# Last tile, one transpose and one load reordered in a fused attention and gated-MLP kernel

## Chip, cores and metric

One core of one Trainium2 chip runs the kernel. The metric is the device time of one execution in microseconds (us), lower is better. Before the change: 230.65 us, median of 3 (230.29 to 230.92). The span in a profile runs from the first to the last instruction, about 1.7 us less than the time. A program on one core has no second die to compare with, so a run of several is called slow only when it is over 1.5% above the fastest of its kernel.

## The reference

```python
x = A_x                                  # 2048 x 512, bf16
xn = layernorm(x)
# attention: 32 heads of 16, each position looks at 8 positions, 2 apart, backwards
q, k, v = split(xn @ A_wqkv)             # 512 x 1536
s = window_attention(q, k, v) @ A_wo     # 512 x 512
g = silu((gelu(xn @ B_w_gate) * (xn @ B_w_up)) @ B_w_down)   # 512 -> 1792 -> 512
return x + s * g
```

(Shortened: the mask of the first positions, the reshapes and the scale are left out.)

## The kernel before

The kernel works on four blocks of 512 rows (j = 0 to 3), each of four tiles of 128 rows. A block is normalized and transposed, projected to q, k and v, goes through attention on VectorE and the gate, up and down products on TensorE. Everything is issued by hand in an order that keeps TensorE busy. All DMAs are issued by one engine, SyncE, from one queue.

The loads at the start, and the late weights.

```python
for t in range(TPQ):                       # TPQ = 4
    load_x(t)
for i in range(3):
    load_w(wqkv_sb, A_wqkv, i * D, (i + 1) * D)      # q, k, v weights
load_x(TPQ, TPQ)
# ... gate and up weights, the other x tiles ...

def load_late_weights():
    nc.sync.dma_start(out=wd_sb[:], in_=B_w_down.rearrange("(k p) n -> p k n", p=P))
    for g in range(NC):
        nc.sync.dma_start(
            out=wo_sb[:, g, :],
            in_=bass.AP(
                tensor=A_wo.tensor, offset=g * 4 * D, ap=[[D, 4], [DH * D, H], [1, D]]
            ),
        )
```

Tiles 4 to 6 are transposed by TensorE during the first gate-and-up products, tile 7 by DMA. Then the queue loads v and the late weights:

```python
for i in range(TPQ):
    # ...
    if i < TPQ - 1:
        at(("glu", 0, i), transpose, TPQ + i)
# ...
at(("glu", 0, 0), transpose_by_dma, 2 * TPQ - 1)
at(("glu", 0, 0), load_v, 0)
at(("glu", 0, 0), load_late_weights)
```

The softmax reciprocals of blocks 0 to 2 go through DRAM, to be spread over the partitions, and are waited for by the division:

```python
def spread_by_dma(j):
    nc.sync.dma_start(out=rs_d[j][:, :], in_=st[j]["rs"][:])      # store
    rb = op.tile([P, TQ], BF16, name="rbd")
    for i in range(WL):                                           # four loads
        nc.sync.dma_start(
            out=rb[H * i : H * (i + 1), :].rearrange("h (q i) -> h q i", q=4),
            in_=rs_d[j].rearrange("(q h) i -> h q i", h=H),
        )
    st[j]["rb"] = rb
# divide(j): oT = o * rb on VectorE; down(j, tt): y = h @ wd, then s = oT @ wo
```

The last tile works by halves of the columns: y, Silu, s, multiply, add, store, twice. (Tiles named `_ps` lie in PSUM, the memory into which TensorE sums.)

The softmax here doesn't subtract the row's maximum and nothing guards it: scores larger than these inputs give would overflow.

## Time and profile before

| What | Before | How to read it |
|---|---|---|
| span | 228.8 us | first to last instruction |
| TensorE busy | 97% | the bound; VectorE 65%, ScalarE 57% |
| first q projection | 7.15 us | end of the head |
| first y and second y product of block 0 | 57.67, 61.55 us | between them is the first s product, which needs the division |
| last matmul starts | 225.24 us | end of TensorE's work |
| last store issued, landed | 226.40, 227.93 us | the tail |

The prediction shows the lines of these views: the page's busy shares and the chain that ended last, TensorE's waits, and the timelines of the head, of the queue and of the tail. The chain is followed back from the last instruction, at each step to what released it. An increment is a step of the semaphore by which a DMA says that a share of it has landed.

### The profile page before, as it was taken

The page shows a single profiled execution, that of the slowest core. Times are in us where ns is not written, and L with a number is a line of the kernel's source. Part 1 is how long each engine was busy: PE and PEld are TensorE (multiplying, and loading weights), DVE is VectorE, ACT ScalarE, POOL GpSimd, SP SyncE. Part 2 cuts the span into 40 slices and gives each one's busy share as a digit, 9 for nine tenths or more (in the row PEclk, how much of TensorE's full clock was granted, in tenths as well). Part 3 has the DMA queues.
Part 4 walks back from the last instruction along what each step waited for, and adds up shares of the span by engine and source line. Part 5 has one row for each costly group of instructions (what it writes and reads, how often), then busy time and mean ns, then how long its engine had stood idle before and what let it go on. Part 6 is the DMA issues. An engine that isn't in the chain of part 4 may idle for free.

```text
span 228.8 us, 3516 instructions
## 1 busy us (share of the span) xinstructions
PE 222.7 (97%) x1303; PEld 106.8 (47%) x1323; DVE 147.6 (65%) x234; ACT 130.6 (57%) x215; POOL 21.7 (10%) x61
## 2 busy tenths in 40 slices
PE   7999999999999999999999999999999999999994
PEld 5865444444444444444444444444444444444453
DVE  4593996894898198865678169735449429845232
ACT  3679779764514867476721687646741387647211
POOL 1048944100000000110000000000000000000000
PEclk9999999999999999999999999999999999999999
DMA  6999599922366611110266711110038910000001
GB/s 157 357 375 376 140 175 199 315 98 80 91 153 152 135 23 29 27 29 0 92 162 152 162 29 23 26 34 6 30 104 193 202 30 3 0 0 4 23 23 46
DMA packets 29857, 24.33 MB, mean 106 GB/s; under 512 B 9488, under 2 KB 29840, under 8 KB 29840
## 3 DMA queue, kind: packets, MB, share of 16 engines
q1 hardware_dynamic: 29840, 24.11, 41.0%
q8 instruction: 10, 0.16, 0.3%
q14 instruction: 7, 0.06, 0.1%
HBM read 18.61 MB, written 4.31 MB: 100 GB/s over the span
## 4 chain that ended last, share of the span: by engine, by line
PE 94%; ACT 2%; DVE 1%; DMA 1%; issue 1%; ACTq 0%; DVEq 0%
PE y_ps L411 21%; PE u_ps L242 21%; PE g_ps L242 20%; PE qkv_ps L242 17%; PE s_ps L421 6%; PE L_ps L299 3%; PE o_ps L370 3%; DMA x_sb<-in_A_x_dram 1%; PE q_ps L242 1%; PE tr L208 1%; DVE stats L177 1%; ACT L395 1%; ACT u L397 1%; PE den_ps L319 0%; ACT xnT L217 0%
## 5 line engine op out<-in xcount | busy, mean ns | idle before, releaser
L242 PE MATMUL u_ps<-xnT,wu_sb 128*128 128x512 bf16 x223 | 57.3, 379 | 0.2
L242 PE MATMUL g_ps<-xnT,wg_sb 128*128 128x512 bf16 x214 | 56.5, 379 | 0.6 <-issue 0.2
L411 PE MATMUL y_ps<-wd_sb,h 128*128 128x512 bf16 (+1 forms) x234 | 50.9, 366 | 0.2
L399 DVE TENSOR_TENSOR h<-ge,u 128x512 bf16<-128x512 bf16 x56 | 23.8, 424 | 37.5 <-ACT u L397 36.8
L288 DVE TENSOR_TENSOR pk<-q_sb,k_sb 128x2048 bf16<-128x2048 bf16 x32 | 37.8, 1221 | 7.0 <-ACT k_sb L263 7.0
L395 ACT ACTIVATE ge<-g_ps 128x512 bf16<-128x512 f32 x56 | 33.6, 600 | 14.7 <-PE g_ps L242 14.0
L397 ACT ACTIVATE u<-u_ps 128x512 bf16<-128x512 f32 x56 | 33.6, 599 | 14.6 <-PE u_ps L242 14.4
L242 PE MATMUL qkv_ps<-xnT,wqkv_sb 128*128 128x512 bf16 (+1 forms) x203 | 40.5, 354 | 0.2
L356 DVE TENSOR_TENSOR pv<-E,v_arr 128x2048 bf16<-128x2048 bf16 x32 | 38.6, 1217 | 0.0
L411 PEld LDWEIGHTS <-h 128*128 128x128 bf16 x238 | 23.3, 98 | 25.3
L418 ACT ACTIVATE sl<-y_ps 128x512 bf16<-128x512 f32 (+1 forms) x17 | 9.7, 573 | 44.0 <-PE y_ps L411 44.0
L242 PEld LDWEIGHTS <-wu_sb 128*128 128x128 bf16 x224 | 21.9, 98 | 26.6 <-issue 0.3
L242 PEld LDWEIGHTS <-wg_sb 128*128 128x128 bf16 x224 | 21.2, 98 | 26.8 <-issue 3.0
L242 PEld LDWEIGHTS <-wqkv_sb 128*128 128x128 bf16 x224 | 21.7, 98 | 19.6 <-issue 0.4
L429 DVE TENSOR_TENSOR m<-s_ps,sl 128x512 bf16<-128x512 f32 (+1 forms) x17 | 11.2, 658 | 22.4 <-PE s_ps L421 22.4
L421 PE MATMUL s_ps<-wo_sb,oT 128*128 128x512 bf16 (+1 forms) x68 | 16.6, 366 | 0.0
L193 POOL TENSOR_TENSOR rstd<-rstd,mhalf 128x1 f32<-128x1 f32 x12 | 7.7, 638 | 78.9 <-DVE rstd L190 76.7
L266 ACT ACTIVATE vst<-qkv_ps 128x512 bf16<-128x512 f32 x16 | 9.6, 598 | 6.4 <-PE qkv_ps L242 6.4
L263 ACT ACTIVATE k_sb<-qkv_ps 128x512 bf16<-128x512 f32 (+1 forms) x20 | 10.2, 517 | 3.4 <-PE qkv_ps L242 3.2
L260 ACT ACTIVATE q_sb<-qkv_ps 128x512 bf16<-128x512 f32 (+1 forms) x16 | 8.7, 545 | 3.5 <-PE qkv_ps L242 3.3
L421 PEld LDWEIGHTS <-oT 128*128 128x128 bf16 x68 | 6.6, 98 | 7.2
L382 DVE TENSOR_TENSOR oT<-o_ps,rbd 128x1024 bf16<-128x1024 f32 x6 | 7.1, 1219 | 3.7 <-PE qkv_ps L242 3.7
(52 smaller groups left out, 119.3 us busy)
## 6 DMA issues: line engine op xcount, KB each, us to landing
v_arr<-vT SPq DMA_DIRECT2D x16, 520.0 KB, 5.1
vT<-vst SPq DMA_DIRECT2D x16, 128.0 KB, 2.8
out_dram<-o_t SPq DMA_DIRECT2D x15, 128.0 KB, 2.3
wg_sb<-in_B_w_gate_dram SPq DMA_DIRECT2D x2, 896.0 KB, 10.8
wu_sb<-in_B_w_up_dram SPq DMA_DIRECT2D x2, 896.0 KB, 10.9
wd_sb<-in_B_w_down_dram SPq DMA_DIRECT2D x1, 1792.0 KB, 16.9
wqkv_sb<-in_A_wqkv_dram SPq DMA_DIRECT2D x3, 512.0 KB
x_sb<-in_A_x_dram SPq DMA_DIRECT2D x3, 512.0 KB, 11.6
```

What stands on the lines that cost most here:

```text
L242: nc.tensor.matmul(ps, lhsT=w[:, dk, lo : lo + P], rhs=xnT[j][:, dk, i0 : i0 + n], start=(dk == 0), stop=(dk == NC - 1),)
L263: nc.scalar.activation(out=k_sb[:, c, lo : lo + n], in_=ps, func=AF.Copy)
L266: nc.scalar.activation(out=vst[:], in_=ps, func=AF.Copy)
L288: nc.vector.tensor_tensor(out=pk[:], in0=st[j]["q"][:], in1=k_sb[:, :, off : off + TQ], op=ALU.mult)
L356: nc.vector.tensor_tensor(out=pv[:], in0=st[j]["E"][:, wh, :].unsqueeze(1).to_broadcast([P, 4, TQ]), in1=st[j]["va"][:, 4 * g : 4 * g + 4, ...
L395: nc.scalar.activation(out=ge[:], in_=g_ps[:], func=AF.Gelu_apprx_tanh)
L397: nc.scalar.activation(out=u[:], in_=u_ps[:], func=AF.Copy)
L399: nc.vector.tensor_tensor(out=h[:], in0=ge[:], in1=u[:], op=ALU.mult)
L411: nc.tensor.matmul(y[:], lhsT=st[j][fc][:, tt * P : (tt + 1) * P], rhs=wd_sb[:, fc, cols], start=(fc == 0), stop=(fc == NF - 1),)
L418: nc.scalar.activation(out=sl[:, cols], in_=y[:], func=AF.Silu)
L421: nc.tensor.matmul(s[:], lhsT=st[j]["oT"][:, g, tt * P : (tt + 1) * P], rhs=wo_sb[:, g, cols], start=(g == 0), stop=(g == NC - 1),)
L429: nc.vector.tensor_tensor(out=m[:], in0=s[:], in1=sl[:, cols], op=ALU.mult)
```

## The change

The intent: the last s product no longer stands after the last y, so that less work follows the last matmul; four fewer transposes on TensorE; and the q weights, which the first projection needs, come before x tile 3, which is needed later. Four more warm-up matmuls fill the wait before the first transpose. The core of the diff:

```diff
-    for t in range(TPQ):
+    for t in range(TPQ - 1):
         load_x(t)
-    for i in range(3):
+    load_w(wqkv_sb, A_wqkv, 0, D)
+    load_x(TPQ - 1)
+    for i in range(1, 3):
         load_w(wqkv_sb, A_wqkv, i * D, (i + 1) * D)
...
-        xn = xns[t] = sm4.tile([P, D], BF16, name="xn")
+        xn = xns[t] = xnp.tile([P, D], BF16, name="xn")     # 6 buffers instead of 4
...
+        else:                                               # the last tile
+            s = sm2.tile([P, D], BF16, name="s_last")
+            nc.scalar.activation(out=s[:], in_=attention_product(j, tt)[:], func=AF.Copy)
+            for i in range(2):
+                cols = slice(i * D // 2, (i + 1) * D // 2)
+                finish(s, down_product(j, tt, cols), cols)
...
-        if i < TPQ - 1:
+        if i < 2:
             at(("glu", 0, i), transpose, TPQ + i)
...
     warm_up(17, TQ // 2)
+    warm_up(4, P)
...
-    at(("glu", 0, 0), transpose_by_dma, 2 * TPQ - 1)
+    at(("glu", 0, 0), transpose_by_dma, TPQ + 2)
     at(("glu", 0, 0), load_v, 0)
+    at(("glu", 0, 0), transpose_by_dma, TPQ + 3)
     at(("glu", 0, 0), load_late_weights)
```

More of the change, by code (lines that the diff above doesn't have):

```diff
@@ L68 @@
     sm4 = pool("sm4", 4)
+    xnp = pool("xnp", 6)
     dram = pool("dram", 1, space=bass.MemoryType.DRAM)
@@ L400, in glu, with down_product, attention_product @@
         st[j][fc] = h
+    def down_product(j, tt, cols):
+        y = mm.tile([P, cols.stop - cols.start], F32, name="y_ps", tag="mm")
+        for fc in range(NF):
+            nc.tensor.matmul(
+                y[:],
+                lhsT=st[j][fc][:, tt * P : (tt + 1) * P],
+                rhs=wd_sb[:, fc, cols],
+                start=(fc == 0),
+                stop=(fc == NF - 1),
+            )
+        return y
+    def attention_product(j, tt):
+        s = mm.tile([P, D], F32, name="s_ps", tag="mm")
+        for g in range(NC):
+            nc.tensor.matmul(
+                s[:],
+                lhsT=st[j]["oT"][:, g, tt * P : (tt + 1) * P],
+                rhs=wo_sb[:, g, :],
+                start=(g == 0),
+                stop=(g == NC - 1),
+            )
+        return s
@@ L402, in down @@
     def down(j, tt):
         t = j * TPQ + tt
-        halves = [slice(0, D // 2), slice(D // 2, D)] if t == NT - 1 else [slice(0, D)]
-        n = D // len(halves)
         sl = sm2.tile([P, D], BF16, name="sl")
         o_t = sm4.tile([P, D], BF16, name="o_t")
-        for i, cols in enumerate(halves):
-            y = mm.tile([P, n], F32, name="y_ps", tag="mm")
-            for fc in range(NF):
-                nc.tensor.matmul(
-                    y[:],
-                    lhsT=st[j][fc][:, tt * P : (tt + 1) * P],
-                    rhs=wd_sb[:, fc, cols],
-                    start=(fc == 0),
-                    stop=(fc == NF - 1),
-                )
-            nc.scalar.activation(out=sl[:, cols], in_=y[:], func=AF.Silu)
-            s = mm.tile([P, n], F32, name="s_ps", tag="mm")
-            for g in range(NC):
-                nc.tensor.matmul(
-                    s[:],
-                    lhsT=st[j]["oT"][:, g, tt * P : (tt + 1) * P],
-                    rhs=wo_sb[:, g, cols],
-                    start=(g == 0),
-                    stop=(g == NC - 1),
-                )
-            m = sm2.tile([P, n], BF16, name="m")
-            nc.vector.tensor_tensor(out=m[:], in0=s[:], in1=sl[:, cols], op=ALU.mult)
@@ L430, in down, with finish @@
+        def finish(s, y, cols):
+            nc.scalar.activation(out=sl[:, cols], in_=y[:], func=AF.Silu)
+            if s is None:
+                s = attention_product(j, tt)
+            m = sm2.tile([P, cols.stop - cols.start], BF16, name="m")
+            nc.vector.tensor_tensor(out=m[:], in0=s[:, cols], in1=sl[:, cols], op=ALU.mult)
             nc.vector.tensor_tensor(out=o_t[:, cols], in0=m[:], in1=x_sb[:, t, cols], op=ALU.add)
             nc.sync.dma_start(out=out2d[t * P : (t + 1) * P, cols], in_=o_t[:, cols])
+        if t < NT - 1:
+            cols = slice(0, D)
+            finish(None, down_product(j, tt, cols), cols)
+        else:
[4 more added lines that the diff above has]
+                finish(s, down_product(j, tt, cols), cols)
```

## The prediction

> **What bounds the kernel now.** I read the page first for the bound, then who waited for whom, then the chain of waits in order of time, then the timeline at each place that the change touches: the head, the first gate-and-up products, the DMA queue behind them, and the tail.
>
> ```profile
> PE 222.7 (97%) x1303; PEld 106.8 (47%) x1323; DVE 147.6 (65%) x234; ACT 130.6 (57%) x215; POOL 21.7 (10%) x61
> ...
> PE 94%; ACT 2%; DVE 1%; DMA 1%; issue 1%; ACTq 0%; DVEq 0%
> ```
>
> TensorE is busy for 97% of the 228.8 us span, and 94% of the chain that ended last is TensorE. The second largest engine stands at 65%. So only two kinds of edit can pay: fewer TensorE instructions, or a shorter head or tail.
>
> ```profile
> PE warm_ps L225 <- DVE k_sb L162: 1.1, 1, 1.1
> PE tr L208 <- DVE xn L199: 0.3, 1, 0.3
> PE g_ps L242 <- issue: 0.2, 1, 0.2
> ```
>
> These are all the waits of TensorE that the profile lists, 1.6 us, and 1.4 of it lies before 5.3 us. There is no large wait in the body to remove.
>
> The head, from the timeline (start, duration, engine, line, operation):
>
> ```profile
> 6.41 0.66 DVE L177 BATCH_NORM_STATS2 stats<-x_sb 128x6 f32<-128x512 bf16 x1
> ...
> 6.71 0.66 ACT L217 ACTIVATE xnT<-tr 128x256 bf16<-128x256 bf16 x2 [0.26 <-PE tr L208]
> ...
> 6.92 1.85 PEld L242 LDWEIGHTS <-wqkv_sb 128*128 128x128 bf16 x16
> ...
> 7.15 1.91 PE L242 MATMUL q_ps<-xnT,wqkv_sb 128*128 128x256 bf16 x16
> ```
>
> The first real matmul, at 7.15, needs the copy of transposed tile 1 (its first half ends at about 7.1) and the q weights. The trace's record of semaphore increments has the q weights complete at 6.88, and the first of their loads into the array starts at 6.92. So the weights are second by 0.2 us, and the copy is what holds the q projection in this execution.
>
> The transpose of tile 6 stands in the chain of waits in the middle of the first gate-and-up products:
>
> ```profile
> 21.28 1.02 PE u_ps L242 x4
> 22.30 0.22 PE tr L208 x4
> 22.53 0.86 PE g_ps L242 x4
> ```
>
> The queue that issues DMAs, in that stretch:
>
> ```profile
> 21.57 6.09 SPq L234 DMA_TRANSPOSE xnT<-xn  x4
> 27.83 2.65 SPq L276 DMA_DIRECT2D v_arr<-vT  x4
> 30.53 0.67 SPq L105 DMA_DIRECT2D wd_sb<-in_B_w_down_dram  x1
> 31.24 14.42 SPq L107 DMA_DIRECT2D wo_sb<-in_A_wo_dram  x4
> ```
>
> Today four transposes of tile 7 take the queue 6.1 us, then v, then the late weights. From the increments: the four pieces of v are complete at 33.2, 35.9, 38.6 and 42.7, the down weights at 47.5.
>
> The tail:
>
> ```profile
> 224.91 0.60 PE L421 MATMUL s_ps<-wo_sb,oT 128*128 128x256 bf16 x4
> 225.11 0.39 ACT L418 ACTIVATE sl<-y_ps 128x256 bf16<-128x256 f32 x1 [1.58 <-PE y_ps L411]
> 225.62 0.43 DVE L429 TENSOR_TENSOR m<-s_ps,sl 128x256 bf16<-128x256 f32 x1 [1.21 <-PE s_ps L421]
> 226.08 0.29 DVE L430 TENSOR_TENSOR o_t<-m,x_sb 128x256 bf16<-128x256 bf16 x1
> ```
>
> Silu of the last half (225.11 to 225.49) runs entirely beside the four s matmuls, so it costs nothing today. What follows the last matmul is the multiply out of PSUM and the add.
>
> **What the Trainium skill says.** "TensorE: Matmul & The Clock Gate", Part 1 (What's actually happening): the array runs at half rate until a free-running window of about 3.4 us has been busy. The trace agrees: the clock record grants full speed from 6.86 us; warm-ups of 256 columns are 0.213 us apart before, q matmuls of 256 columns 0.109 us after. It was granted although TensorE idled from about 4.72 (0.213 after the last warm-up's start at 4.50) to 5.21. "DMA: Bandwidth & Descriptors", Queues, rings and completion order: on each DMA engine, descriptors are consumed in ring order. The trace agrees: v and the down weights complete in the order of issue. "VectorE: DVE Perf Modes", What auto-detection actually checks: two results a cycle need every tensor 16-bit. The trace agrees: 256 columns take 0.43 us with an f32 operand in PSUM, 0.29 us all in bf16 in SBUF.
>
> **The change, part by part.**
>
> *Tile 6 by DMA.* Despite its words, tile 7 goes by DMA already (36 transposes by DMA = 9 tiles of 4); only tile 6 is new. Four TensorE transposes go, 0.22 us of the chain (four starts 0.055 us apart). One 0.65 us ScalarE copy goes too, at 23.04, where TensorE waited for nothing. The wait just before (the second u_ps product held by the first Gelu, whose table load takes 1.28 us at 19.34) concerns tiles 4 and 5 and stays. Nothing later is tied to absolute time, so the gain should last to the end: -0.22 us.
>
> The price is in the DMA queue. Tile 6 takes tile 7's old place, so v keeps its times. Tile 7's four transposes follow, at about 30.5 to 36.6, behind v in the rings, so they land after v is complete at 42.7. Moving one takes little: today three of them completed 0.19 us apart, so four are done by about 42.7 + 0.8 = 43.5. The projection that needs them starts at 45.03, or 44.8 after the gain: 1.3 us to spare. The down weights slip from 47.5 to about 48.3, needed at 57.8; the output weights finish about 0.8 us later too, needed at 60.8. All hidden. The pool of six buffers for the normalized tiles keeps tile 11's normalization, at 42.9, from waiting for tile 7's late transposes.
>
> *q weights ahead of x tile 3, and four more warm-ups.* The queue issues a load about every 0.47 us, and 128 KB at the 377 KB per us that the sixth microsecond moved is 0.35 us. So the q weights should land 0.35 to 0.45 us earlier, near 6.5, and x tile 3 where the weights end today, 6.5 to 6.9 instead of 5.06. In the profiled execution the first gains nothing, since the copy holds the matmul until 7.1. In executions whose clock is released before about 5.2 the transposes run twice as fast, the copies end near 6.6, and then the weights at 6.9 hold it: up to 0.3 us. But most of that is taken back. The statistics of tile 3 start at about 6.8 instead of 6.41, and on VectorE they stand before the normalization of tile 2, which ends at 8.20 (7.79 + 0.41) and slips to about 8.6. Its transpose follows the 16 q matmuls, at 8.89 today, so it can't be earlier than 8.6 to 8.65. The warm-ups, at 0.107 us each, fill 4.72 to 5.14, before the normalized tile is ready at 5.17: they delay nothing, and as the window was accepted with the gap in it, I expect nothing from them. Together: 0 to -0.3, taken as -0.1 us.
>
> *The last tile.* The arithmetic on TensorE is the same: 4 matmuls of 512 columns (4 x 0.216 = 0.86) in place of 8 of 256 (8 x 0.109 = 0.87). But the last y half now ends where the last s half ended before, and Silu, hidden before, stands behind it. The y matmul that starts last starts at about 225.23. Silu follows 0.31 later, as today (224.80 to 225.11): 225.54 to 225.92. Multiply from SBUF at 0.29, from about 225.97 to 226.26; add, 226.30 to 226.59. Today it ends at 226.37. So +0.22 us: the multiply saves 0.14, Silu and its handover cost the rest. ScalarE's copy of s, 0.6 us, lies beside the y matmuls.
>
> Sum: -0.22 - 0.1 + 0.22 = -0.1 us, so 230.55 us.
>
> **The rivals.** *Tile 7's transposes come late.* For it: they queue behind v, the slowest load of that stretch, with an estimated 1.3 us of slack. Against it: v's times were set by work that does not change. If v slipped by 2 us, the projection would wait 0.7 us: about 231.2 us. *The tail gains.* If Silu and the multiply turn out to overlap more than I work out, or the s copy frees something that I don't see, the last part would bring 0 to -0.2 rather than +0.22: about 230.2. Against it: the rows above put Silu beside the s matmuls already. *The head gains fully.* If the added warm-ups bring the full clock one window earlier more often and the weights no longer hold the q projection, up to 0.5 us: about 230.1. Against it: the normalization of tile 2, as above. *Tile 3 comes later than 7.3*: then its statistics hold tile 2's transpose beyond 8.9, and the head loses 0.2 to 0.4: about 231.0.
>
> **Range and chances.** All steps are tenths of a microsecond, and the three timings of before already spread over 0.63 us. The rivals reach from 230.1 to 231.2, so 230.0 to 231.1 should hold it 8 times in 10. Two per cent is 4.6 us, ten times any step: faster 0.01, the same 0.98, slower 0.01.
>
> **What would show it.** Right: 24 TensorE transposes instead of 28 and 40 by DMA; q weights complete near 6.5; the first projection of the second block starting without a wait, about 0.2 us earlier relative to the first u_ps product; the last Silu starting 0.3 us after the last y matmul's start, with multiply and add of 0.29 us each behind it, and the final store issued about 1.4 us after that start (today 1.16 us after the last s matmul's start at 225.24). Wrong: TensorE idle before 45 us with tile 7's transposes as its releaser, an idle stretch before tile 2's transpose near 8.9, or a final store earlier after the last matmul than today.

## The result, and the profile after

The changed kernel takes 230.76 us, median of 6 (230.27 to 230.94), against 230.43 us for the kernel before (6 runs). The ratio is 1.0008, 95% interval 0.9995 to 1.0022: the same. A ratio is the mean time of one kernel's fast runs over that of the other's of the same rounds, so not quite the ratio of the medians. The time lies in the predicted range, 0.2 us from its centre. But several steps of the working were wrong, and they cancelled.

The page of the changed kernel, busy shares and chain:

```profile
PE 222.3 (97%) x1299; PEld 106.1 (46%) x1319; DVE 147.4 (64%) x234; ACT 130.7 (57%) x215; POOL 22.7 (10%) x61
...
PE 71%; DMA 14%; SPq 8%; DVE 4%; issue 1%; ACT 1%; DVEq 0%; ACTq 0%
```

TensorE's busy share is unchanged, but it makes only 71% of the chain, where it made 94%. Now 22% is DMA and the queue that issues DMAs. That does not mean that 22% of the time is lost to DMA; it says that one thing which TensorE waited for late came from a long line of transfers. TensorE's waits say which:

```profile
PE warm_ps L228 <- DVE k_sb L165: 1.1, 1, 1.1
PE s_ps L420 <- DVE oT L385: 0.5, 1, 0.5
PE q_ps L245 <- ACT xnT L220: 0.3, 1, 0.3
```

The second line is new: an s product waits for the division `oT`. (The list has 0.5 us, because a matmul's modelled end, 0.38 us after its start, comes later than the next start could, 0.22 us after; the s product itself takes 0.70 us longer.) The chain before it, in order of time (start, duration, what):

```profile
50.72 4.85 DMA rs_d<-rs
...
55.59 0.33 SPq L350
...
56.91 1.71 DMA rbd<-rs_d
...
59.83 1.23 DVE oT L385
61.06 0.05 issue
61.10 0.60 PE s_ps L420 x2
```

Read from the bottom: the third and fourth matmul of the first s product start at 61.10, when the second half of the division is done. The division had waited for the spread reciprocals, and these for their own store, which took 4.85 us to land. In the kernel before it was issued at 50.92 and landed at 52.74, in 1.82 us. The kernel before, timelines of the queue and of VectorE:

```profile
50.92 0.33 SPq L344 DMA_DIRECT2D rs_d<-rs  x1
52.76 1.75 SPq L347 DMA_DIRECT2D rbd<-rs_d  x4
```

```profile
57.89 2.36 DVE L382 TENSOR_TENSOR oT<-o_ps,rbd 128x1024 bf16<-128x1024 f32 x2 [3.66 <-PE qkv_ps L242]
```

There, too, the division starts when the last spread load has landed (at 57.76 by the increments, later than the releaser that the line names). But it ends at 60.24, 0.88 us before the third s matmul, at 61.12, needs it. That was all the room there was.

The queue that issues DMAs:

```profile
22.37 6.46 SPq L237 DMA_TRANSPOSE xnT<-xn  x4
29.01 2.78 SPq L279 DMA_DIRECT2D v_arr<-vT  x4
31.89 5.11 SPq L237 DMA_TRANSPOSE xnT<-xn  x4
37.05 0.58 SPq L108 DMA_DIRECT2D wd_sb<-in_B_w_down_dram  x1
37.68 10.75 SPq L110 DMA_DIRECT2D wo_sb<-in_A_wo_dram  x4
50.72 0.33 SPq L347 DMA_DIRECT2D rs_d<-rs  x1
55.59 1.75 SPq L350 DMA_DIRECT2D rbd<-rs_d  x4
```

Tile 7's transposes take the queue from 31.89 to 37.00, and the late weights are issued at 37.05 instead of 30.53. By the record of semaphore increments the down weights are complete at 49.94 instead of 47.47, and the last packet of the output weights starts at 54.80 instead of 51.99.

The head and the tail, from the timeline:

```profile
6.64 0.69 DVE L180 BATCH_NORM_STATS2 stats<-x_sb 128x6 f32<-128x512 bf16 x1 [0.23 <-DMA x_sb<-in_A_x_dram]
6.66 1.91 PE L245 MATMUL q_ps<-xnT,wqkv_sb 128*128 128x256 bf16 x16 [0.29 <-ACT xnT L220]
...
7.63 0.41 DVE L202 TENSOR_SCALAR xn<-x_sb,mv,rstd 128x512 bf16<-128x512 bf16 x1
```

```profile
225.53 0.38 ACT L435 ACTIVATE sl<-y_ps 128x256 bf16<-128x256 f32 x1 [1.14 <-PE y_ps L408]
225.94 0.29 DVE L439 TENSOR_TENSOR m<-s_last,sl 128x256 bf16<-128x256 bf16 x1 [0.91 <-ACT sl L435]
226.27 0.29 DVE L440 TENSOR_TENSOR o_t<-m,x_sb 128x256 bf16<-128x256 bf16 x1
```

The q projection starts 0.49 us earlier than before. Tile 3's statistics start 0.23 us later, yet the normalization of tile 2 starts earlier, at 7.63 instead of 7.79. The tail is as predicted: Silu stands alone between the last matmul and the multiply.

One more line, the wait of the queue for the last store, in the stretch from 220 us. The changed kernel:

```profile
SPq L580 <- DMA out_dram<-o_t: 1.2, 1, 1.2
```

The kernel before:

```profile
SPq L558 <- DMA out_dram<-o_t: 0.9, 1, 0.9
```

In both, the last store lands 1.54 us after it was issued. So the queue started to wait earlier in the changed kernel, and the difference lies in what it does after.

The two traces side by side, in us from the start of the span:

| Event | Before | After | Step by step |
|---|---|---|---|
| first q projection starts | 7.15 | 6.66 | head -0.49 |
| first y of block 0 starts | 57.67 | 56.95 | tile 6 another -0.22 |
| second y of block 0 starts | 61.55 | 61.55 | wait before s +0.70, all given back |
| last matmul starts | 225.24 | 225.22 | body equal |
| last store issued | 226.40 | 226.59 | tail +0.21 |
| last store landed | 227.93 | 228.13 | 0 |
| VectorE's last instruction ends | 228.75 | 229.20 | end +0.25 |

So the changed kernel gained 0.71 us, gave 0.70 back in one wait, and lost 0.46 at the end. One profile is one execution, though; the experiments show which of these steps repeat.

### The profile page after: what moved, and what is told of

Its sections match the earlier page's. It is cut to its first block, busy times and chain, and to the rows that moved or that the text cites. A ratio compares the mean times of both kernels' runs of the same rounds, so it can differ in the third digit from the quotient of the medians.

```text
span 229.2 us, 3505 instructions
## 1 busy us (share of the span) xinstructions
PE 222.3 (97%) x1299; PEld 106.1 (46%) x1319; DVE 147.4 (64%) x234; ACT 130.7 (57%) x215; POOL 22.7 (10%) x61
## 4 chain that ended last, share of the span: by engine, by line
PE 71%; DMA 14%; SPq 8%; DVE 4%; issue 1%; ACT 1%; DVEq 0%; ACTq 0%
PE y_ps L408 20%; PE u_ps L245 16%; PE g_ps L245 15%; PE qkv_ps L245 9%; PE s_ps L420 6%; DMA x_sb<-in_A_x_dram 5%; DMA v_arr<-vT 5%; SPq L91 3%; DVE pv L359 3%; PE L_ps L302 2%; PE o_ps L373 2%; DMA rs_d<-rs 2%; SPq L85 2%; SPq L237 1%; SPq L279 1%
## 5 line engine op out<-in xcount | busy, mean ns | idle before, releaser
L245 PEld LDWEIGHTS <-wg_sb 128*128 128x128 bf16 x224 | 21.2, 98 | 27.0 <-issue 3.0
L439 DVE TENSOR_TENSOR m<-s_ps,sl 128x512 bf16<-128x512 f32 x15 | 10.3, 688 | 19.6 <-PE s_ps L420 19.6
L420 PE MATMUL s_ps<-wo_sb,oT 128*128 128x512 bf16 x64 | 16.4, 379 | 0.5 <-DVE oT L385 0.5
L420 PEld LDWEIGHTS <-oT 128*128 128x128 bf16 x64 | 6.1, 98 | 8.4 <-DVE oT L385 1.3
```

The source lines that it names most:

```text
L245: nc.tensor.matmul(ps, lhsT=w[:, dk, lo : lo + P], rhs=xnT[j][:, dk, i0 : i0 + n], start=(dk == 0), stop=(dk == NC - 1),)
L420: nc.tensor.matmul(s[:], lhsT=st[j]["oT"][:, g, tt * P : (tt + 1) * P], rhs=wo_sb[:, g, :], start=(g == 0), stop=(g == NC - 1),)
L439: nc.vector.tensor_tensor(out=m[:], in0=s[:, cols], in1=sl[:, cols], op=ALU.mult)
```

## The experiments

**My theory after the result.** (1) The late weights slip because transposes stand behind v. The output weights run on only 4 of the 16 DMA engines (each of their loads leaves 5 records of increments, the last 4 on landing; every other DMA leaves 16), and the reciprocals' store needs all 16, so it ends with them. (2) The new tail costs 0.2 us. (3) Four more DMAs change which semaphore the last store has, and that costs 0.25 us at the end. (4) The head gains. **Rivals:** the wait comes from the head, from VectorE's order or from the queue itself; the longer end is accidental; the warm-ups make the head's gain.

Twelve kernels ran, in three groups of four; each group shares 11 runs of the kernel before (medians 230.38, 230.54 and 230.50 us). All gave correct results. Effects of 0.2 us are below what the timings resolve.

### Parts alone: tail_only, tile6_only, head_only

`tail_only` is the kernel before with the diff's lines of the last tile alone:

```diff
-        halves = [slice(0, D // 2), slice(D // 2, D)] if t == NT - 1 else [slice(0, D)]
+            nc.scalar.activation(out=s[:], in_=attention_product(j, tt)[:], func=AF.Copy)
+            for i in range(2):
+                cols = slice(i * D // 2, (i + 1) * D // 2)
+                finish(s, down_product(j, tt, cols), cols)
```

> The kernel before with only the new last tile (s first and copied, y by halves). Theory: the last Silu is no longer hidden, so 0.2 us slower: ratio 1.0008 to 1.0012, the last store issued 1.36 us after the start of the last matmul (before: 1.16). Rival (the copy of s frees the end): ratio 0.999 or less and the last store no later after the last matmul than before.

Measured: 230.55 us, ratio 1.0006 (0.9992 to 1.0020), so the timing alone is unclear. In the trace the last store is issued 1.37 us after the start of the last matmul, where all ten profiles with the old tail have 1.16; all four with the new tail have 1.37. The tail costs 0.21 us. The rival, that the copy of s frees the end, falls.

`tile6_only` has the transposes and the buffers alone:

```diff
-        xn = xns[t] = sm4.tile([P, D], BF16, name="xn")
+        xn = xns[t] = xnp.tile([P, D], BF16, name="xn")
-        if i < TPQ - 1:
+        if i < 2:
-    at(("glu", 0, 0), transpose_by_dma, 2 * TPQ - 1)
+    at(("glu", 0, 0), transpose_by_dma, TPQ + 2)
     at(("glu", 0, 0), load_v, 0)
+    at(("glu", 0, 0), transpose_by_dma, TPQ + 3)
```

> The kernel before with only tile 6 moved to DMA (and the six buffers). Theory (the output weights, which 4 of the 16 DMA engines carry, end later, hold the reciprocals' store behind them, and that holds the division): the first y of block 0 starts 0.2 us earlier, but the reciprocals' store lands near 55.5 instead of 52.7, VectorE's division waits for the spread reciprocals (not for TensorE), and the first s product waits, so nothing is left or up to 0.5 us is lost: ratio 1.000 to 1.002. Rival (the wait in the profile after came from the head or from that one execution): the store lands by 53.5 and the 0.2 us stays: ratio 0.999.

Measured: 230.72 us, ratio 1.0015 (0.9996 to 1.0033). The reciprocals' store lands at 54.85. VectorE's wait from 40 to 70 us:

```profile
DVE oT L383 <- DMA rbd<-rs_d: 4.7, 1, 4.7
```

The wait as such is not new (3.4 to 3.8 us in `head_only`, `tail_only`, `qorder_only` and `before_rot4`); what counts is when the division ends: 61.26 us, and 61.05 in the changed kernel, against 60.24 before. From the first to the second y product it takes 4.06 us, where an unhindered execution has 3.88, so 0.18 of the 0.22 us goes back. The wait is smaller than in the changed kernel because here the head did not gain: the less TensorE has gained, the less it waits. The end costs 0.25 us more, as in the changed kernel. The first y is not 0.2 us earlier on the clock, as the q weights were complete only at 7.35 in this execution and the q projection started at 7.39. Relative to the head the gain is there: from the first gate product to the first projection of block 1 it takes 26.55 us in all seven profiles with tile 6 by DMA, and 26.77 in all seven without.

`head_only` has the order of the loads and the warm-ups:

```diff
-    for t in range(TPQ):
+    for t in range(TPQ - 1):
         load_x(t)
-    for i in range(3):
+    load_w(wqkv_sb, A_wqkv, 0, D)
+    load_x(TPQ - 1)
+    for i in range(1, 3):
...
+    warm_up(4, P)
```

> The kernel before with only the q weights ahead of x tile 3 and four more warm-ups. Theory: the reciprocals stay early, so what the head gains (0.1 to 0.5 us, by when the clock is released) is kept to the end: ratio 0.998 to 0.9995, and the first s product has no wait. Rival (the head is bound by the statistics of tile 3 and gains nothing): ratio 1.000.

Measured: 230.43 us, ratio 0.9992 (0.9977 to 1.0007). The q projection starts at 6.76, the first y at 57.28, the second at 61.16 (3.88 apart, no wait), the last matmul at 224.85. So the 0.39 us of the head are kept to the end in this execution, as expected.

### What makes the division late: after_wo16, after_rs_act, tile6_first, before_wo16

`after_wo16` is the changed kernel with the output weights loaded in four pieces of 32 partitions, the same number of DMAs and bytes:

```diff
-        for g in range(NC):
+        for i in range(4):
             nc.sync.dma_start(
-                out=wo_sb[:, g, :],
+                out=wo_sb[H * i : H * (i + 1), :, :],
                 in_=bass.AP(
-                    tensor=A_wo.tensor, offset=g * 4 * D, ap=[[D, 4], [DH * D, H], [1, D]]
+                    tensor=A_wo.tensor, offset=i * D, ap=[[DH * D, H], [4 * D, NC], [1, D]]
```

> The changed kernel with the output weights loaded in four pieces of 32 partitions, which can use all 16 DMA engines, in place of four pieces whose outer size is 4. Theory: the output weights end about 3 us earlier, the reciprocals' store lands within 2.5 us of its issue (4.85 in the changed kernel), the first s product does not wait, and the 0.7 us that head and tile 6 gained is kept: 0.4 to 0.7 us faster than the changed kernel, ratio to before 0.998. Rival (the reciprocals are late for another reason, such as VectorE's order): the wait before the first s product stays and the ratio is 1.0008 as for the changed kernel.

Measured: 230.66 us, ratio 1.0004 (0.9990 to 1.0019). The mechanism is confirmed, the size of the gain is not. The output weights are complete at 51.43, the reciprocals' store lands 1.45 us after its issue, and the division now waits for TensorE:

```profile
DVE oT L385 <- PE o_ps L373: 1.9, 1, 1.9
```

From first to second y it takes 3.88 us: the wait is gone. I had expected 0.4 to 0.7 us off the changed kernel, and the ratios differ by 0.0004, 0.1 us. Part of the miss is mine: I had taken the 0.7 us gained in one profile as typical. And the two kernels ran in different rounds, each with an interval of 0.0014 (0.3 us) to either side, so the timings neither show nor exclude a gain of 0.4 us; that the wait costs time is read from the traces (3.88 us instead of 4.59). The new tail and the longer end, 0.46 us, were still in it as expected.

`after_rs_act` leaves the output weights as they were and issues the reciprocals' store of block 0 from ScalarE's queue:

```diff
-        nc.sync.dma_start(out=rs_d[j][:, :], in_=st[j]["rs"][:])
+        (nc.scalar if j == 0 else nc.sync).dma_start(out=rs_d[j][:, :], in_=st[j]["rs"][:])
```

> The changed kernel with the store of block 0's reciprocals issued by ScalarE, so on another queue than the output weights. Theory (it waits behind the output weights in the same queue): it lands within 2.5 us of its issue instead of 4.85, the first s product does not wait, 0.3 to 0.7 us less between the first y and the second y product than in the changed kernel; end of the kernel as changed, so ratio to before 1.000 to 1.0005. Rival (the DMA engines themselves are too busy, whatever the queue): it lands as late as in the changed kernel.

Measured: 230.93 us, ratio 1.0011 (0.9979 to 1.0043). This expectation failed, and my theory with it in one point: the queue is not the reason. The store was issued at 51.11 from the other queue, and 12 of its 16 increments came at 52.40 to 52.61, but the last four at 54.10, 54.23, 54.25 and 54.81. The last packet of the output weights started at 54.11. In the changed kernel, from the same queue, it was 12 increments by 52.18 and four at 54.79 to 55.57, with the last packet at 54.80. So a store that is spread over 16 engines ends when the 4 engines that carry the output weights are done, whatever queue it comes from. The division ends at 60.92, about as late as in the changed kernel. No wait before s is seen here, because TensorE was late: the head by 0.83 us (q weights complete at 7.44), and another 0.54 us between the first projection of block 1 and the sums `o_ps`. The second is an effect of the edit itself: ScalarE, which now issues the store, waits 2.9 us for the reciprocals before it goes on emptying PSUM. So the time of this run says nothing on the store's queue; the increments do.

`tile6_first` is `tile6_only` with tile 7's transposes before v:

```diff
     at(("glu", 0, 0), transpose_by_dma, TPQ + 2)
-    at(("glu", 0, 0), load_v, 0)
     at(("glu", 0, 0), transpose_by_dma, TPQ + 3)
+    at(("glu", 0, 0), load_v, 0)
```

> Tile 6 alone by DMA, but tile 7's transposes issued before v instead of behind it. Theory (the slip of the late weights came from transposes that follow the loads of v, which end at different times on different engines, so that engines stand idle): the down weights complete by 48.6 us (49.3 with the transposes behind v, 47.5 before), the reciprocals' store lands by 53.8 (54.85), the spread reciprocals a microsecond earlier; the price is v complete near 43 to 44 and a wait of VectorE before the first product with v, up to 0.8 us, hidden from TensorE. End of the kernel with the longer checks (1.07 us after the last landing), ratio 1.0000 to 1.0012. Rival (the slip is the queue's issuing time, which is the same in both orders): down weights at 49 or later again.

Measured: 234.68 us, ratio 1.0174 (1.0141 to 1.0208), by the 2% rule unclear, and far from what I expected. Four of the executions have a mean clock of 0.990 to 0.993, so part of the time may be clock; the profiled one, at clock 1.000, took 233.95 us. Its waits, of TensorE and, from 30 to 75 us, of VectorE:

```profile
PE o_ps L371 <- DVE pv L357: 3.0, 3, 1.5
```

```profile
DVE pv L357 <- DMA v_arr<-vT: 5.0, 1, 5.0
```

I had counted what the transposes move, under a microsecond, and forgotten what they take to issue: 1.2 us each on the queue. The first piece of v is issued at 32.98 instead of 27.67, and v is complete at 47.98 instead of 41.30. VectorE waits 5.0 us for it. What it says on the slip of the late weights is this. The down weights are complete at 52.87, later than 49 as the rival had it, but 5.3 us of that is v's later issue. From the first issue of v to complete down weights it takes 19.6 to 19.8 us in the kernel before and the five others with its transposes and its load of the output weights, and 19.9 us here, where no transpose stands between them either; 20.9 in the changed kernel, 21.4 in `after_rs_act` and 21.6 in `tile6_only`, where four do. (Kernels with the output weights on 16 engines can't be compared: `before_wo16`, below, takes 21.2 without a transpose there, so that edit alone adds 1.6.) So the transposes behind v cost 1.0 to 2.0 us of DMA time, not 0.8.

Where that goes shows in the DMA share (the column before the last) and GB/s (the last) of the stretches from 40 to 44 us. Before:

```profile
41.00:42.00 1.00, 1.00 (x6) 0.42 (x5) 0.93 (x4) 0.68 (x3) 0.00 (x0) 1.00 1.10 323
42.00:43.00 1.00, 1.00 (x6) 0.49 (x5) 0.24 (x2) 0.79 (x2) 0.55 (x1) 1.00 1.10 349
```

After:

```profile
41.00:42.00 1.00, 1.00 (x7) 0.45 (x5) 0.45 (x2) 0.67 (x2) 0.38 (x1) 1.00 2.25 158
42.00:43.00 1.00, 1.00 (x6) 0.43 (x5) 0.75 (x2) 0.67 (x2) 0.17 (x1) 1.00 0.44 71
```

In the changed kernel the rate falls to 71 GB/s for a microsecond in which the down weights were queued. The packets of 256 bytes, which are those of the transposes, have a median of 20 ns there, but the slowest took 1419 ns (64 ns among those of tile 6, which do not follow v). In all six profiles with transposes behind v the slowest takes 798 to 1591 ns; in `tile6_first`, where the same transposes come before v, 62 ns. So the long packets come with the place behind v. That the transposes hold the engines together until the slowest has finished v would fit, but no run tests that.

`before_wo16` is the control: the kernel before, with the edit of `after_wo16`.

> The kernel before with only the output weights on 16 engines. Theory (before has room for late weights): the reciprocals' store lands near 51.9, about a microsecond earlier, VectorE's division waits for TensorE and not for the spread reciprocals, and the time is the same: ratio 0.9992 to 1.0005. Rival (the division was the bound before, too): the first s product earlier relative to the first y, ratio 0.998.

Measured: 230.32 us, ratio 1.0010 (0.9978 to 1.0041; one of six executions took 232.76 us at clock 0.993 and widens the interval). The store lands at 52.21, the division waits 1.8 us for TensorE's sums, and 3.88 us lie between the y products, as before. As expected, the faster load alone buys nothing: the kernel before had room.

### The end of the kernel: before_rot4

`before_rot4` stores tiles 4 to 7 in two halves each: four more DMAs in the middle, no other work.

```diff
-            nc.sync.dma_start(out=out2d[t * P : (t + 1) * P, cols], in_=o_t[:, cols])
+            for r in ((0, P // 2), (P // 2, P)) if 4 <= t < 8 else ((0, P),):
+                rows = slice(r[0], r[1])
+                nc.sync.dma_start(out=out2d[t * P + r[0] : t * P + r[1], cols], in_=o_t[rows, cols])
```

> The kernel before with the stores of tiles 4 to 7 in two halves each: four more DMAs in the middle, no other work. Theory (the loads and stores take eight semaphores in turn; at the end the queue checks them in a fixed order, and 4 more DMAs put the last store's semaphore first instead of last, so the other checks, 0.06 us each, come after it): the last instruction ends 1.07 us after the last store has landed instead of 0.82, span 0.25 longer, ratio 1.0005 to 1.0015. Rival (the longer end of the changed kernel is its own): 0.82 us, ratio 1.000.

Measured: 231.22 us, ratio 1.0041 (1.0002 to 1.0080). Two of six executions took 232.9 and 233.0 us at clock 0.993, and four 230.76 to 231.44 us, so the ratio is above what the edit explains and I don't use it. The trace does decide: the last landing is followed by 1.06 us, not 0.82. Of the six checks of semaphores the last store's is now in the second and not in the last, so that four checks, 0.06 us each, come after the landing. In the changed kernel, too, four come after it. Over all fourteen profiles: the six kernels with 120 DMAs have 0.81 to 0.82 us, the seven with 124 have 1.05 to 1.07, and the one with 128 has 0.80.

### The head: qorder_only, warm_only

> The kernel before with only the q weights ahead of x tile 3, no warm-ups. Theory (the order makes the head's gain, the warm-ups nothing): the q weights complete near 6.2 us instead of 6.9, the q projection starts at 6.65 to 7.1 by when the clock is released, ratio 0.9985 to 0.9998, as with both (0.9992). Rival (the warm-ups make it): q projection at 7.1 or later, ratio 1.000.

Measured (only the order of the loads, the lines of `head_only` without `warm_up`): 230.43 us, ratio 0.9985 (0.9957 to 1.0013). The q weights are complete at 6.17; the clock was released at 6.06, so the projection waited for the copy until 6.96.

> The kernel before with only the four more warm-ups. Theory (they fill TensorE's idle time before the first transpose and nothing else): no idle between warm-ups and first transpose, the q projection still waits for its weights near 6.9 or the copy at 7.1, ratio 0.9990 to 1.0010. Rival (they bring the clock earlier and so the head's gain): q projection at 6.7 or earlier, ratio 0.998 to 0.999.

Measured (only `+    warm_up(4, P)`): 230.35 us, ratio 0.9990 (0.9977 to 1.0004). In its profile the clock was released at 7.00, later than in the kernel before although the idle time was filled, and the q projection waited for its weights until 7.79. So warm-ups did not help that execution; what they do on average is open, since neither timing is clear.

The fourteen profiles together say more on the order. Seven have the old order: q weights complete at 6.75, 6.86, 6.88, 6.97, 7.19, 7.35 and 7.74, mean 7.11. In six of them the projection starts within 0.06 us of that; the seventh is the profile that I predicted from. Seven have the new order: mean 6.49, and the first gate product starts at 18.03 on average instead of 18.30. The new order is worth about 0.3 us, with a spread as large as itself.

### A version that beats both: best_rot4 and best_plain

`best_plain` is the changed kernel with the old last tile and the output weights on 16 engines. `best_rot4` adds the four halved stores, so that it has 128 DMAs and the last store its old place among the eight semaphores.

> All that gains and nothing that costs: the new head, tile 6 by DMA, the output weights on 16 engines, the old last tile, and four stores in halves so that the last store has its old place among the eight semaphores. Theory: head -0.2 to -0.4, tile 6 -0.22, nothing given back: ratio 0.997 to 0.999, and 0.82 us from the last landing to the end. Rival (something else takes the gain): ratio 1.000 or more.

Measured: 229.92 us (229.71 to 230.31), ratio 0.9966 (0.9938 to 0.9994), clear of 1. (One of the 11 runs before in this group, which `qorder_only` shares, took 232.43 us at clock 0.993. Without it the ratios of the means are 0.9975 here, still clear of 1 by my arithmetic, and 0.9994 for `qorder_only`.) In its trace the first y starts at 56.91 and the second at 60.79, 3.88 apart; the last matmul starts at 224.47; 0.80 us follow the last landing. From the timeline around the first s product:

```profile
55.29 2.36 DVE L385 TENSOR_TENSOR oT<-o_ps,rbd 128x1024 bf16<-128x1024 f32 x2 [1.86 <-PE o_ps L373]
...
59.93 1.03 PE L424 MATMUL s_ps<-wo_sb,oT 128*128 128x512 bf16 x4
```

The division starts at 55.29 and is done over 2 us before the s product needs it; the changed kernel's started at 58.69.

> The best version without the four halved stores: new head, tile 6 by DMA, output weights on 16 engines, old last tile. Theory: as the best version up to the last landing, then 1.07 us to the end instead of 0.82, so 0.25 us slower than it: ratio to before 0.9975 to 0.9985. Rival (the place of the last semaphore is worth nothing): the same as the best version, 0.9966, with 0.82 us.

Measured: 230.34 us (230.19 to 230.54), ratio 0.9993 (0.9980 to 1.0006), slower than I expected (0.9975 to 0.9985), with 1.05 us after the last landing. It is 0.42 us above `best_rot4` by the medians, of another group and another chip. Of this the end explains 0.25. In its profile the k weights, complete at 8.86, held TensorE for 0.3 us more. So the halved stores are worth 0.25 us by the traces, and the 0.42 is not all theirs.

## Why the prediction was right, and where not

The number was right: 230.76 us is inside 230.0 to 231.1, and the class is the same. Point by point:

- **Tile 6, -0.22 us on TensorE: right.** 24 transposes instead of 28, and the first y product gained 0.22 us over what the head had gained (26.55 instead of 26.77 us from the first gate product to block 1, in seven profiles against seven). Wrong was that the gain should last to the end because "nothing later is tied to absolute time"; the next point says what was. The projection that needs tile 7 did not wait, but nearly all of its slack was gone: tile 7's four transposes, one for each quarter of the contraction, landed at 43.66, 43.91, 44.16 and 44.41 (predicted: all by 43.5). The projection started at 44.32, reads the last quarter some 0.65 us later (three matmuls of 0.216 us), and no wait of TensorE is listed there.
- **"All hidden", of the late weights: the step that failed.** I checked when the down and output weights themselves are needed, which was right, and not what shares their engines. The slip was mis-sized, too: 0.8 us predicted for the down weights, 2.5 measured, of which 1.2 is v being issued later in that execution (29.01, the latest of the thirteen profiles that issue it there) and the rest the transposes behind v; in `tile6_only` and `after_rs_act` the slip was 1.8. The output weights then hold 4 engines for over 5 us, the reciprocals' store ends with them at 55.57, and the division, which had 0.88 us of room, ends at 61.05 and takes back 0.70 us. None of my rivals named this. `after_wo16` shows it by removing it.
- **The head, 0 to -0.3: direction right, working wrong.** I predicted from an execution in which the copy held the projection. In six of seven profiles with the old order the weights did. And the step by which tile 3's statistics take most of it back failed: the normalization of tile 2 ended earlier, at 8.04 instead of 8.20. In the profile before, ScalarE's square roots for tiles 2 and 3 stood behind its copies of the transposed tiles and ended at 7.74; I had charged the whole 1.79 us from the statistics to the end of the normalization to VectorE. Measured: about -0.3 us on average, -0.49 in the profile after.
- **The tail, +0.22: right.** +0.21 in the changed kernel and in `tail_only`, with the multiply at 0.29 us and Silu 0.31 us after the last y matmul's start.
- **Not seen at all: the end.** +0.25 us because 124 DMAs instead of 120 put the last store's semaphore ahead of four other final checks. `before_rot4` shows it alone.

So -0.1 predicted was -0.7 gained (one profile), 0.70 given back and 0.46 lost at the end. That the number came out near is luck: the prediction had neither the give-back nor the end. Part of it has a cause: TensorE waits at one point for something whose time it does not set. The division ends at 60.92 to 61.26 in the three profiles with transposes behind v and the output weights on 4 engines, whatever the head gained, and what TensorE gains beyond that disappears there. What stays open: why exactly transposes behind v cost up to 2.0 us, and what the warm-ups do.

**The chip's page that I had and did not use.** The Trainium skill, "DMA: Bandwidth & Descriptors", Why a DMA increments its semaphore by 16 and not by 1, says that the number of engines is the largest up to 16 that divides the slowest dimension of both sides. With an outer size of 4 that is 4 engines. The trace agrees: from 49 to 54 us hardly anything but the output weights moves, at 91 to 94 KB per us (apart from the microsecond with the reciprocals' store), where the down weights have about 350, a quarter. The same page, Queues, rings and completion order, says that a semaphore increment lands only after every earlier write of that engine, across its queues. The four late increments of `after_rs_act` agree with it, but do not need it: there the store's own data came late (last section).

## What to carry to other kernels

When a transfer slips, ask not only when its data is needed but which later transfer shares its engines: a small store over 16 engines is as late as the slowest 4. A gain ahead of a wait for something whose time the gain does not move is kept only as far as there is room before that wait (0.88 us before the change; with the changed kernel's division, and TensorE at its old times, 0.07), so look for the next such wait, and its room, before adding gains up. And a change of a few tenths of a microsecond should be judged on several profiles: here the one at hand was the exception in seven.

## What the Trainium skill lacked or had wrong

- "DMA: Bandwidth & Descriptors", Queues, rings and completion order, says that an engine takes turns between queues packet by packet, a packet being several descriptors. No such turn shows in `after_rs_act`, with the reciprocals' store on ScalarE's queue: 96 of its 128 pieces of 256 bytes started at 51.96 to 52.23, but the 32 for the four busy engines only at 53.43 to 53.54 (24) and 54.16 to 54.26 (8), the latter after the last piece of the output weights (54.11). How many descriptors made a packet the trace does not show, so this leaves open whether the page is wrong.
- No page gives what one DMA transpose of 128x128 bf16 from SBUF to SBUF costs the issuing queue: mostly 1.1 to 1.3 us each here (four in 5.11 us), though it moves only 32 KB. Putting four of them ahead of a load delayed that load by 5.3 us.
- No page says that transposes behind loads which end unevenly slow the DMA engines: single packets took up to 1419 ns (median 20 ns; at most 62 ns where the transposes came before the loads) and the rate fell to 71 GB/s with weights queued. The cause is not settled here.
- No page says that the end of a kernel depends on how many DMAs it has: with eight semaphores in turn, 120 or 128 DMAs left 0.80 to 0.82 us after the last landing, 124 left 1.05 to 1.07.
